# Another order of the same 2043 operations, and another choice of VectorE or GpSimd for them

## The chip, the core and the metric

The kernel runs on one core of a Trainium2 chip. The time is the device time of one execution in microseconds; lower is better. The core has five engines with a queue each: TensorE (PE, with its weight loads shown as PEld), VectorE (DVE), ScalarE (ACT), GpSimd (POOL) and SyncE (SP, which issues the DMAs here). Each runs its own instructions strictly in the order in which the program lists them, and waits on semaphores where it needs another engine's result.

## What is computed

A recurrent attention over 768 tokens (4 batches, 8 heads, head size 40), whose output goes through a soft mixture of 8 experts. All data are float32.

```python
def _attn_ref(r, k, v, w, a, b) -> np.ndarray:
    B, H, S, D = r.shape
    state = np.zeros((B, H, D, D), dtype=np.float32)
    y = np.zeros_like(r)
    for t in range(S):
        ...
        y[:, :, t] = np.einsum('bhd,bhde->bhe', rt, state)
        Sa = np.einsum('bhde,bhe->bhd', state, at)
        state_decay = state * wt[:, :, None, :] - np.einsum('bhd,bhe->bhde', Sa, bt)
        state = state_decay + np.einsum('bhd,bhe->bhde', vt, kt)
    return y.astype(np.float32)

def _moe_ref(x, phi, w1, w2) -> np.ndarray:
    ...
    logits = x @ phi
    d = logits - logits.max(0, keepdims=True)
    d = np.exp(d)
    d /= d.sum(0, keepdims=True) + 1e-09
    slot_input = d.T @ x
    ...
    for e in range(E):
        h = np.maximum(slot_input[e] @ w1[e], 0.0)
        slot_out[e] = h @ w2[e]
    ...
    return (c @ slot_out).astype(np.float32)
```

## The kernel before

The 768 tokens are cut into 12 stages of 64, and every two stages form a pair. Inside a stage the recurrence is turned into matrix products, and only the state goes from stage to stage.

- Preparation of a stage (scan_s, scan_k, scan_c): two scans along the tokens, which VectorE alone can do here, and three 768-wide products of two SBUF operands on either VectorE or GpSimd.
- Grams (lgram, gram, gram_0): TensorE multiplies, VectorE masks the result out of PSUM.
- Solve of a pair (solve_in, solve_step, solve_out): the inverse of triangular 32x32 blocks. VectorE transposes the blocks, ScalarE copies them, and then 30 steps follow, each with a product and a sum over SBUF operands of 30 to 240 elements a partition. Each instruction needs the result of the one before. One buffer (n_a, lt_a) serves all pairs, so a solve starts only after the one before has been transposed out. The first pair is solved in another way (solve_half, VectorE alone); five pairs use solve_step, 300 instructions in all, each on VectorE or GpSimd.
- Chain of a stage (chain_g, chain_u, chain_s): TensorE carries the state on. chain_u of the first stage of a pair needs the solve of that pair (pairs writes it to tbs, of which there is one).
- Output of a stage (y_ut, y_sd, y_p, y_y) and, for each pair, the logits and the running softmax of the experts' slots (slots_a to slots_e); at the end the experts' two products and the output.

The program first records all operations without running them. Then four strings, the result of a search, decide: ORDER gives each recorded operation its place in the program (two digits to base 64 each), and so the order on every engine; PICK gives, for each operation or team of operations that two engines can do, the first or the second of them (VectorE or ScalarE, VectorE or GpSimd); BANK gives each PSUM tile one of eight banks; PACED makes a load wait for another load.

```python
        for os_, c in zip(self.teams(), "".join(PICK)):
            for o in os_:
                o.eng = list(o.alt)[int(c)]
        two = lambda t: [64 * DIGITS.index(t[i]) + DIGITS.index(t[i + 1]) for i in range(0, len(t), 2)]
        rank = two("".join(ORDER))
        self.order = [o for _, o in sorted(zip(rank, self.ops), key=lambda x: x[0])]
```

A step of the solve, as it is recorded:

```python
            nc.both.tensor_tensor(
                tv, n_t[:, 0:i, i:i + 1].broadcast_to([128, i, m]),
                lt[:, i:i + 1, i + 1:].broadcast_to([128, i, m]), ALU.mult)
            nc.both.tensor_tensor(n_t[:, 0:i, i + 1:], n_t[:, 0:i, i + 1:], tv, ALU.add)
```

In the profile every instruction carries the line of emit (L1178), so groups are told apart by engine, operation, tile and shape. A 128x30 to 128x240 TENSOR_TENSOR of wt tiles is a step of a solve; 120x768 is a product of the preparation; 120x780 and 120x781 scans are those of scan_c and scan_s; STREAM_TRANSPOSE is solve_in or solve_out.

Of the kernel before, what the change touches and what calls it, by code (L numbers as in the profile page):

```python
# [124 lines left out]
ORDER = (
    "Cu0203070904100005010F060I0H0G0K0J0E0R0S0A0B0C0V0U0Z0Y0W0X0a0b0h0c0d1d0f0l0e0m0N0L0M0Q1V0O0k0g1a1-1z212O1+2N1j1k"
    "221b1Z0T0i0j0n0o0s0z0u3N1u3K0t0y0p0q0r081P1X1v1q1r0w1f0+0-1l241m1o1t262511122A2C2Z2a2m2b2c2j13140x1i2B2F1g1h0v1c"
    "151628292o2p2n272G1718191A2R0D2T2P2Q0P1n1s2d2e1B1C2x331p2h1D1E1F1G2-1H1I2f2i3D2+3Z1J1K2H2g4S4v1L1M2y1N1O1Q1R2z36"
    "2E2W1S2X2I2l3738393C2J2K2Y3135346T7C5G5v2D2k322w2v4O4Q4M4q3S3o3T3r3A3V4u3B3E5H5u4Y4d5i5tAj631y1Y1e3P3Q3W3X3Y4E3R"
    "2r2L1T2t232U2u3b3p2V4k2q3F3O303j4-3H3L3a4C3U3q3I3J5U3d3e3f3g3c3k4g204h1U4e2M4j1W4i1w6V3h3i3l3m4D4F4I4G4J4H4P3n3s"  # L130
    "4W4b3t3u4f4X4c3v3w3x3y4R4T3z3+4U4n6i3-4041424344454647485N5I5L494A601x6Z6U6a2s565C4K4L3G3M4N4a4l4r4t5l4V4Z6g5O5P"
    "6K5j714m4p4o4w59585B5A575J5k6A4y516O6P6x6w5D5E5M4s4x4z6S7u4B4+50525354555T6G6N5V5W6W6c5y5X5Y6-705Z5a5b5c5R5r5m5q"
    "5n5p5o5d5e696X7B5f5g6m6n6o6p6H6J6q6r6Q6R6s6t6u6v727D7G7H7I686L6Y7f7z6B6E6I78797765675z64615+666b5-2S8B747A6C6D6F"
    "6l6k6j916d88629B9D999G7U7V5K5S5h5x757E7F7N5s5w7M7Q7d9I7L7c5F5Q6M6y6z7R7b7X7Z7a7S7T7i7t767O7g7w737JA0937K7j7y6h6+"
    "7P7h7v8C8R8-6f8H7x8h7e7l9V7+808182837-847m8T9F8F8f7W7Y8S8g8m7k9E8W8i8j8+8d8Y8D856e8789978A8G86APAT9A9+8a8k8l8E95"
    "949890AD92BQBfB1B6BRBS8b8c8e8z8n8p9CAFBcBdBo8V8ZAHA7AAAcAGAd8U8X8oA19JA5ANBp9H9z9w9x9v9yAMALBOBqC1CAA4ACA2AyB0B5"
    "AIAJDoCUCoDqAEAKAW9-A8A9BHBI7n7o7p7q7r7s8I8J8K8LDtDuEb8M8N8O8P8Q8q8r8sAhAxAm96AO8t8u8v8w8x8y9K9LA3A-9M9N9O9P9Q9R"
    "9S9TAXAaAbAYAZAtAv9U9WABA+Be9X9Y9Z9aEhEoEqGY9b9c9d9e9f9g9h9i9j9kB9BA9l9mA6AV9n9o9p9q9r9s9t9uBlBtBuBsBmAwAzB8EREc"
    "IXB-C0BDBEBPIYJHKnNjBMBUBLASARAiAeAqArAfApAQAoCZB3BKBNBYBZAUCcAkCdAnCaAlEOEPBbBnB4BFAsAuBTBVBWBkBrBgB2B7BhAgBGC+"
    "BiBvB+C3BBBCBJCBCHCGCFCECfC-CCCLC2C7BxByBwC9CzEdBjCICJBXBaC4CvDzCDCTCWCVE0CgCmBzC5DgChD4D2CiD1DnD3DxEKF6CyEGEMEZ"  # L140
    "DrDyD+CKCeE9EBECETEVEWCbE5CYCXE6E1E8E3D-FaFRE+FAEAEFEHE7FcE2FdE4FeFYENEQF7FKELEXD0DpCxD5EIESEUFEEyF1GEDsDvFGEkEn"
    "GzFFFHCwDwEDEEEJEgEuGIEfEtEwExF2EvFJFCFDF8GGGPEYElEsFBEiEjFyFzH4GkGlGvH2F3F4F5EaEmEeEpErC6C8CMCNCOCPCQCRCSCjJ0J8"
    "KACkClCnCpCqCrCsCtFnFxFkFjFhD6D7D8D9DADBDCDDEzF0DEDFDGDHDIDJDKDLF9FIFMFPFQFLFODMDNE-FZFNDODPDQDRJQJRJaJcDSDTDUDV"
    "DWDXDYDZDaDbFUFVDcDdFoG8DeDfDhDiDjDkDlDmG9GMGLGVGNFpF+F-K0JgKgMYG6G7G0G1G4KFKmNVONFwFvGHFWFXFbFlFiFuFtFTFSIHIBGi"
    "GmG2G3GCFsIgFgIhFfIFFmG5GZIzJ6GAGBGJGKGTGUGDGSGaGRFqFrGQITIUJOGFGWH7HAGcGfGgGeGsGoGqGpH3GrINItGnGyG-IvG+H5IxIuGt"
    "GuH6GdGjIKGhGxILIsICIGIJGOGwGXGbHaHBIOIPIQISH+HzIVIWKDIMIaH1H9I-J9JDH8IRJBJEJIJ1J7IZIkIDIfIpIiImIIIqIlIjJkJCJbIc"
    "IwJAIrJtIoJmJiJGInH0J5JTJUIdJ3IyJ4I+J2JMJWJZK4KHKRK-IbIeK1JSJzJyJXK8KqKsJKJNJPJJJVLNJdJhK6K7JeKEJfK2K3KzLKLOJwKM"
    "KJKOKIKPKGK9LULcLdMEMHKZKbKeJLJxJ-JYKNHCHDHEHFHGHHHIHJHKHLMQN9MXHMHNHOHPHQHRHSHTLILYJFJvJsHUHVHWHXHYHZHbHcKKKLHd"
    "HeHfHgHhHiHjHkKtKxKvKyL2L7KwHlHmJ+K5KCHnHoHpHqMxNDNNPiHrHsHtHuHvHwHxHyH-I0KWKlI1I2LRLTI3I4I5I6I7I8I9IAL3L4L9L6L5"
    "LJLXLZNYMINbMZK+LPLSLeLfQ2R8SBSCKTKSKQJjJnJrJqJpJlJuJoKBMgLDL0L8LFLGLHMAMTLxM1L-M3KVKdL1LWKULyLzKaLLLMKXKjKrKuLa"  # L150
    "LhLiM0M6M7M9M8M5M4KYKhMBMSKcKpMLMWMJMKMMLbLgMCKfKkMuMyMjMpLBKiKoLQLVOpMNN8NANBMwMvMPNKNPL+MDNONQNTNJNMNRNSNZMlMk"
    "MrMsMnMqMoMmMtO5O9NHNoNWNXNaLAN-O2O1MhMeLCLEMfMdMbMcM2N7NFNfNLNcNUNdMONCNENlNmPTPUPXNGNINnOGNeNiNpNwOFPbNrNtNvNu"
    "NsOKOOPSPZPdNxOPNqOMPjQ0Q1Q3QINkNyOHNgNhOLLjLkLlLmLnLoLpLqLrLsQOQoR3LtLuLvLwMFMGMRMUOWP3O4O8O0MVMaMzM+M-N0N1N2N3"
    "N4N5N6OZOaObOcOIOVOJOTOSOkOUOROdOeOfOgOhOiPkQEQFQrOjOlOmOnOoOrOsOtOuOvOQPEOwOxOyOzO+O-P0P1P2PLPOPPPgQQQJPDPMPNRC"
    "QHRyRlOYPFPIRKSST1TSODOEP9PAP8OBO6P7OCPmPBP4PGPHIEMiROQcQeQYOXP5PKPYPVPWPfOqP6NzO3N+Q6O7OAPcPtPJPQPaPlPyPzPrPqQG"
    "PpPeQyPvP-PwP+Q4PCPoPsQPQRQ7Q8QWQKQVQNQTQLPRQMQUQ5QDQ+Q-R5QlQnQpQAQbQ9QZQCQBQaQXQdRURNR0R1R9QgQhQjQsR4RARHR7RFRG"
    "QkQmPuQSQvR2QxQqQtRdRLRhRgRjRiRfReQiRIRkR6RJQzRERqRmRuS5SFRDRnRoQuQwRBSOSUSLRbRvS8ThSzSWSjRZS9SERsRwRxS7RaRtSwS6"
    "TFSdSJSKSRSTRRRTS2RSRYRQRPS1RXRcS0TcRrS3R+SDRpSQT9TfSMSPTdQfTXTYPnRMSASHSVSYSXPhPxRzTsR-S4SgSeSlSGSISySNSfSZSbSh"
    "SoSsT0SkSnSiSmTZUMRWUZRVTaUNTbUbTeTgTiTkTzSpSrSuSaScT2TjSqSvSxStS+S-T7T3T4T5T6TtTvU3UYT8TDTETGTITJTATBTHTNTCTOTK"
    "TLTPTQTRTTTUTVTlTmTMTrUBUCUFUHUUUVTWU7U6U4U5U8TnTpTqT+T-UKU9UQURTuTyUAUSUDULTwToTxU0U1UEUIUGUJU2UOUXUWUTUPUaVTVU"  # L160
    "VWUfUgUjUkUlUcUdUeUhUiUmUnUoUpVKUqVBUrUvUyUtUxUwUzU-U+ViV0V4V5UuV1V6V8UsV2V3V9VQVSVRVAVGVbVVVYVLVsVoVpV7VCVFVXVt"
    "VuVwVvVIVOVDVEVJVNVHVMVPVcVaVjVdVeVkVlVZVfVgVhVnVmVqVr"
)
# [1278 lines left out]
```

## Time and profile before

| | us |
|---|---|
| median of 3 runs | 405.3 |
| lowest and highest of them | 404.92, 413.21 |
| the profiled execution | 405.49 |
| its span, first to last instruction | 403.7 |

| engine | busy us | share of the span |
|---|---|---|
| TensorE | 337.1 | 84% |
| VectorE | 295.4 | 73% |
| ScalarE | 189.4 | 47% |
| GpSimd | 199.4 | 49% |

The profiled execution's own time is 1.8 us above its span. The mean granted clock of TensorE was 0.916 of its upper level. Busy shares are means over the whole span; what holds the end is read from the chain of waits and from windows of a stretch.

### The profile page before, as it was taken

How to read it: one execution, taken by the hardware profiler on the slowest of the kernel's cores; microseconds unless marked ns; L12 is line 12 of the kernel's file. 1: busy time of each engine (PE TensorE's matmuls, PEld its weight loads, DVE VectorE, ACT ScalarE, POOL GpSimd, SP SyncE). 2: the span in 40 equal slices, each digit the busy share in tenths (PEclk: the TensorE clock that was granted, in tenths of full speed). 3: DMA queues.
4: the chain of work that ended last, by engine and by line, in shares of the span. 5: the costliest groups of instructions: out<-in, count | busy, mean ns of one | idle time of the engine just before them, and what ended most of it. 6: DMA issues, size and time to landing. Idle time of an engine off the chain costs nothing.

```text
span 403.7 us, 18293 instructions
## 1 busy us (share of the span) xinstructions
PE 337.1 (84%) x8097; PEld 295.6 (73%) x8097; DVE 295.4 (73%) x563; ACT 189.4 (47%) x399; POOL 199.4 (49%) x280
## 2 busy tenths in 40 slices
...
GB/s 186 262 233 113 210 3 97 53 188 147 203 54 107 170 92 120 83 64 229 45 62 145 157 182 237 142 157 232 225 169 248 207 203 208 312 296 13 3 175 215
...
## 3 DMA queue, kind: packets, MB, share of 16 engines
...
## 4 chain that ended last, share of the span: by engine, by line
PE 38%; POOL 31%; DVE 13%; issue 8%; DMA 4%; ACT 2%; SPq 0%; DVEq 0%; POOLq 0%; ACTq 0%
PE ps L1178 38%; POOL wt L1178 31%; DVE wt L1178 11%; DMA wt<-in_kb_dram 3%; ACT wt L1178 1%; DMA wt<-in_ww_dram 1%; ACT mem L1178 1%; DVE ps L1178 1%; DVE mem L1178 1%; DVE mid L1178 0%; SPq L1178 0%; DVE slx L1178 0%; DVE old L1178 0%; ACT mid_r L1178 0%; DMA mem<-in_rd_dram 0%
## 5 line engine op out<-in xcount | busy, mean ns | idle before, releaser
L1178 POOL TENSOR_TENSOR wt<-wt 128x234 f32<-128x234 f32 (+14 forms) x237 | 151.4, 639 | 85.9 <-DVE wt L1178 38.0
L1178 PE MATMUL ps<-wt,wt 120*32 120x96 f32 (+9 forms) x3432 | 149.8, 246 | 32.3 <-POOL wt L1178 17.3
L1178 PEld LDWEIGHTS ps<-wt,wt 120*32 120x32 f32 (+7 forms) x3432 | 134.6, 135 | 42.4 <-POOL wt L1178 17.5
L1178 ACT ACTIVATE wt<-ps 32x320 f32<-32x320 f32 (+1 forms) x129 | 55.4, 429 | 30.5 <-PE ps L1178 28.8
L1178 PE MATMUL ps<-cs_t,wt 120*128 120x120 f32 (+4 forms) x448 | 65.3, 284 | 2.5 <-DVE wt L1178 1.7
L1178 DVE TENSOR_TENSOR wt<-ps,cs_t 128x512 f32<-128x512 f32 (+2 forms) x96 | 56.8, 612 | 10.1 <-PE ps L1178 9.6
L1178 ACT COPY wt<-ps 128x320 f32<-128x320 f32 (+2 forms) x81 | 39.5, 507 | 41.4 <-PE ps L1178 38.3
L1178 PEld LDWEIGHTS ps<-cs_t,wt 120*128 120x128 f32 (+4 forms) x448 | 49.5, 148 | 7.2 <-DVE wt L1178 2.4
L1178 DVE TENSOR_TENSOR_SCAN wt<-wt,wt 120x781 f32<-120x781 f32 (+1 forms) x24 | 46.1, 1926 | 2.2 <-DMA wt<-in_ww_dram 1.6
L1178 PE MATMUL ps<-mem 64*64 64x40 f32 (+2 forms) x648 | 41.1, 253 | 5.0 <-DVE wt L1178 4.0
L1178 PE MATMUL ps<-wt,mem 64*64 64x40 f32 (+3 forms) x1072 | 40.1, 254 | 3.6 <-issue 1.7
L1178 PEld LDWEIGHTS ps<-wt,mem 64*64 64x64 f32 (+3 forms) x1072 | 36.6, 135 | 7.5 <-issue 3.3
L1178 DVE TENSOR_TENSOR wt<-wt 128x108 f32<-128x108 f32 (+19 forms) x91 | 34.3, 377 | 10.0 <-POOL wt L1178 7.6
L1178 POOL TENSOR_TENSOR wt<-wt,wt 120x768 f32<-120x768 f32 x17 | 34.4, 2033 | 9.3 <-DMA wt<-in_aa_dram 4.3
L1178 DVE STREAM_TRANSPOSE wt<-wt 128x1024 f32<-128x1024 f32 x12 | 24.8, 2068 | 18.7 <-POOL wt L1178 17.4
L1178 ACT ACTIVATE wt<-wt,bm_t 120x768 f32<-120x768 f32 (+1 forms) x35 | 29.0, 861 | 12.1 <-POOL wt L1178 4.0
L1178 PEld LDWEIGHTS ps<-mem 64*64 64x64 f32 (+2 forms) x648 | 26.8, 141 | 9.7 <-DVE wt L1178 5.0
L1178 PE MATMUL ps<-mem,wt 40*64 40x64 f32 x1536 | 29.0, 228 | 0.3 <-DVE wt L1178 0.2
L1178 PEld LDWEIGHTS ps<-mem,wt 40*64 40x64 f32 x1536 | 26.4, 142 | 2.7 <-issue 1.2
L1178 ACT COPY mem<-ps 120x480 f32<-120x480 f32 (+4 forms) x45 | 18.1, 408 | 20.6 <-PE ps L1178 11.8
L1178 DVE TENSOR_TENSOR wt<-wt,wt 120x768 f32<-120x768 f32 x20 | 23.8, 1198 | 0.2 <-DMA wt<-in_kb_dram 0.2
L1178 DVE TENSOR_TENSOR ps<-ps,wt 120x480 f32<-120x480 f32 (+1 forms) x30 | 17.8, 602 | 6.7 <-PE ps L1178 6.7
...
## 6 DMA issues: line engine op xcount, KB each, us to landing
...
```

The source lines that it names most:

```text
L1178: nc.gpsimd.memset(ysb, 0.0)
```

## The change

The operations are the same, and so is the program that records them. The four strings are others, found by a search in which VectorE and GpSimd exclude each other where both use SBUF operands. Read against the recorded operations, the choice of engines changes as follows:

| operations that can go to two engines | before | after |
|---|---|---|
| solve_step, VectorE / GpSimd | 63 / 237 | 141 / 159 |
| products of scan_k and scan_c, VectorE / GpSimd | 20 / 16 | 16 / 20 |
| small products of scan_s, VectorE / GpSimd | 8 / 3 | 6 / 5 |
| two products ahead of stage 0 and 1, VectorE / GpSimd | 0 / 2 | 2 / 0 |
| copies out of PSUM and the like, VectorE / ScalarE | 75 / 357 | 51 / 381 |

Of the solve's instructions 109 go from GpSimd to VectorE and 31 from VectorE to GpSimd. Within the five solves the engine changes from one instruction to the next 10, 6, 7, 2 and 17 times before, and 24, 18, 23, 17 and 23 times after.

```diff
 ORDER = (
-    "Cu0203070904100005010F060I0H0G0K0J0E0R0S0A0B0C0V0U0Z0Y0W0X0a0b0h0c0d1d0f0l0e0m0N0L0M0Q1V0O0k0g1a1-1z212O1+2N1j1k"
-    "221b1Z0T0i0j0n0o0s0z0u3N1u3K0t0y0p0q0r081P1X1v1q1r0w1f0+0-1l241m1o1t262511122A2C2Z2a2m2b2c2j13140x1i2B2F1g1h0v1c"
...
+    "G7040800060E6a010M0C05020A0703090B0N0K0D0G0R0T0b0l0m0i0e0p0L0Y1I0f0q1i0v0x0y0u0I0F0J0P0H0O100+0t0c0r0k0S0o0j1715"
+    "1o2B0U0V0s0-0z1214181y2e1O2+161C13191B0Z1Y1W1n1w231A1c1E1G2A2H2X1v1z2P2Z1H1J1r1-2K2S2W2l2r2t1M1N1D1f1d1q2V2k1a1t"
...
 )
 PICK = (
-    "1111111011101011111110111110111111111111101110111111111111111011110110000110111100000010111111111111111101110111"
-    "1110100111101111111111011111111111111111111111111101100111011111111111111111111011111100111111110000100000111111"
-    "0001011111111111101111111111111111111111111111101111111011111011010111001111101111111101111110011001110001000100"
-    "0000011111111111111111110111111111111111111111111111101111101101111011110011101111111111111110111111001111111110"
-    "0010111111111111111111111111111011111111111111111111111111101111110111101111100111000111001011001001111111101110"
-    "0010100001001111111111111111111111111001101011111100101110100101110100111100010010101011011111001111101110110011"
-    "0000001110000"
+    "0101110010101101111111011111111111111010111111111111110111111011101111110111110000011110110100000111001111110111"
+    "0100000101011100011110011101111111101111111111111111101111101111111111011011111011111100111111110110101111000000"
+    "1100001110001110001001111111001110110111111110111111111111110111111111111111111111111111111111111011110010010000"
+    "1111001110000100001011000101000101101011111001111111111111111111111111110111111111111111111111111101001111111111"
+    "0101111001001010000000000001100011101111111100011110111000011111111111111111110101101011111111111101111111100000"
+    "1110001000110000010001110110101001111100101011110001110110011110101111111111010101011111010010111011110001100101"
+    "1000001110110"
 )
 BANK = (
-    "0124330665270356725170002715272651376477011662725022576356353677314002527664236431054353014141760614503307542036"
...
+    "0123032642556636667713201556560431036327414106527427466406422205234437637525166377126617752503677012532211450413"
...
 )
 PACED = (
-    "------------------------------------------------------------------1f--------------------------------------------"
-    "0g------0v--0s--0v0i----------------0s----0y130w1B1F1210--1M181Q0+19120z101J0y11141Z1N111P1E1S1G1D1E1a1R1Z1V1Z1f"
...
+    "----------------------------------------------------------------------------------------------------------------"
+    "--------0b----0m--0v0v----0v0z0q--0b0k------0w171E11--140+1I101A1J0i0i1E111J1J1K1P121Z0y1N1E1M1G1F1V1l1L1a1c1b1Z"
...
 )
```

## Rows read from the trace of the kernel before

**Rows 1.** The page's first part: busy time and share of the span by engine.
```profile
PE 337.1 (84%) x8097; PEld 295.6 (73%) x8097; DVE 295.4 (73%) x563; ACT 189.4 (47%) x399; POOL 199.4 (49%) x280
```

**Rows 2.** The page's chain that ended last, share of the span by engine.
```profile
PE 38%; POOL 31%; DVE 13%; issue 8%; DMA 4%; ACT 2%; SPq 0%; DVEq 0%; POOLq 0%; ACTq 0%
```

**Rows 3.** Windows: stretch, length, busy time of PE PEld DVE ACT POOL, PEclk, DMA.
```profile
60.00:99.40 39.40, 36.80 (x1004) 33.39 (x1004) 31.12 (x59) 24.82 (x51) 30.29 (x47) 1.00 0.51 120
99.40:110.70 11.30, 8.75 (x158) 8.12 (x151) 9.12 (x8) 7.67 (x15) 3.27 (x3) 0.70 0.78 190
110.70:152.60 41.90, 39.37 (x1091) 36.76 (x1079) 34.82 (x60) 24.71 (x51) 33.66 (x50) 0.96 0.43 106
152.60:160.00 7.40, 5.92 (x124) 5.07 (x122) 6.88 (x8) 3.96 (x7) 0.00 (x0) 1.00 0.35 105
160.00:202.40 42.40, 37.73 (x950) 34.24 (x946) 32.50 (x63) 25.61 (x55) 34.14 (x49) 1.00 0.40 107
202.40:209.70 7.30, 4.77 (x136) 4.24 (x140) 6.80 (x8) 4.34 (x8) 0.03 (x1) 0.50 0.04 10
209.70:257.80 48.10, 44.88 (x1044) 41.01 (x1038) 34.82 (x65) 25.91 (x56) 38.23 (x57) 0.90 0.69 185
257.80:267.60 9.80, 7.42 (x140) 6.65 (x144) 8.62 (x13) 5.57 (x10) 0.02 (x1) 0.83 0.43 129
267.60:303.10 35.50, 33.77 (x941) 30.17 (x933) 27.01 (x67) 13.96 (x34) 22.72 (x47) 1.00 0.73 200
```

**Rows 4.** Waits of TensorE, 60 to 303 us: total us, times, longest.
```profile
PE ps L1178 <- DVE wt L1178: 12.4, 8, 6.0
...
PE ps L1178 <- POOL wt L1178: 2.5, 1, 2.5
```

**Rows 5.** Timeline, TensorE: the same 32 matmuls of chain_u in two stages.
```profile
158.02 1.13 PE L1178 MATMUL ps<-wt,mem 64*64 64x40 f32 x32
...
209.81 1.89 PE L1178 MATMUL ps<-wt,mem 64*64 64x40 f32 x32
```

**Rows 6.** Chain that ended last, 84 to 93 us: start, length, what.
```profile
86.31 0.58 POOL wt L1178
86.89 0.07 issue
```

**Rows 7.** Timeline, GpSimd and VectorE, 80 to 89 us.
```profile
80.01 0.62 POOL L1178 TENSOR_TENSOR wt<-wt 128x238 f32<-128x238 f32 x1 [0.52 <-DVE wt L1178]
...
86.72 1.81 DVE L1178 TENSOR_TENSOR_SCAN wt<-wt,wt 120x780 f32<-120x780 f32 x1
...
86.96 1.96 POOL L1178 TENSOR_TENSOR wt<-wt 128x210 f32<-128x210 f32 x1
```

**Rows 8.** Groups by form, GpSimd, all of the span: count, busy us, mean ns, idle before.
```profile
L1178 POOL TENSOR_TENSOR wt<-wt 128x238 f32<-128x238 f32 x19 | 19.1, 1004 | 2.4 <-DVE wt L1178 1.0
...
L1178 POOL TENSOR_TENSOR wt<-wt 128x210 f32<-128x210 f32 x16 | 14.5, 904 | 6.3 <-DVE wt L1178 5.3
...
L1178 POOL TENSOR_TENSOR wt<-wt 128x198 f32<-128x198 f32 x14 | 8.0, 571 | 1.1
```

**Rows 9.** Groups by form, VectorE, 60 to 303.1 us.
```profile
L1178 DVE TENSOR_TENSOR wt<-wt,wt 120x768 f32<-120x768 f32 x17 | 18.4, 1090 | 0.2 <-DMA wt<-in_kb_dram 0.2
L1178 DVE STREAM_TRANSPOSE wt<-wt 128x1024 f32<-128x1024 f32 x8 | 16.5, 2067 | 18.6 <-POOL wt L1178 17.4 <-ACT mem L1178 1.2
...
L1178 DVE COPY mem<-ps 120x480 f32<-120x480 f32 x5 | 3.1, 623 | 0.0
...
L1178 DVE TENSOR_TENSOR wt<-wt 128x198 f32<-128x198 f32 x6 | 2.2, 363 | 0.1
```

**Rows 10.** Timeline, the output's DMA issues.
```profile
385.16 14.64 SPq L1178 DMA_DIRECT2D out_dram<-wt  x24
```

**Rows 11.** Waits of VectorE, 60 to 303 us.
```profile
DVE wt L1178 <- POOL wt L1178: 25.3, 14, 6.9
DVE wt L1178 <- PE ps L1178: 10.4, 12, 2.6
```

More of the change, by code (lines that the diff above doesn't have):

```diff
@@ L131 @@
[L131 to L150, printed above, removed]
@@ L161 @@
-    "VWUfUgUjUkUlUcUdUeUhUiUmUnUoUpVKUqVBUrUvUyUtUxUwUzU-U+ViV0V4V5UuV1V6V8UsV2V3V9VQVSVRVAVGVbVVVYVLVsVoVpV7VCVFVXVt"
-    "VuVwVvVIVOVDVEVJVNVHVMVPVcVaVjVdVeVkVlVZVfVgVhVnVmVqVr"
+    "G7040800060E6a010M0C05020A0703090B0N0K0D0G0R0T0b0l0m0i0e0p0L0Y1I0f0q1i0v0x0y0u0I0F0J0P0H0O100+0t0c0r0k0S0o0j1715"
+    "1o2B0U0V0s0-0z1214181y2e1O2+161C13191B0Z1Y1W1n1w231A1c1E1G2A2H2X1v1z2P2Z1H1J1r1-2K2S2W2l2r2t1M1N1D1f1d1q2V2k1a1t"
+    "1P1Q2E2G2b2n2g1F1L1R1T1U1V2L0g2Y0W2M0Q2x32363B1X1b2q3G1K2a1e1g1j1k2w1m1p2u2-3Q4T4q1s1u22314V4Z1x1+2v202124252y34"
@@ new lines @@
+    "1h2h262R292U2c2z3I3K2J2T303A3C3L5e5r4G4N1l3335383D404K3s4-393r2s373J3U3p3H3O3E3S4L4b4D4I2D2d0h1S1Z3N3W3b3Z3Y3c3j"
+    "2j2o0w2m2C2F0X42492O4F2I3d3k3F3M3f3V4f3h3i3a3v3R3e733m3n3o3q3X3P450n472N4J0d4B0a11282i3u3y46483l413w3-3z433t4C4H"
+    "444E4M4P3T4O4a4R4U4W4Y4X4e4d4g3g4x6M4j4l4u585F5J5L5P5T5X5M5G5V5a5d4v2f5K2p545g6j745R6K5A6G3x4Q4h4m4p6V4A4S6S3+4i"
+    "5x6L6i4c4k4t4r5E4+525059565h5y4y556f7I7O63535I5S4o4w5B606F5i5l5o5s5u5z61665q67696D515U5Z6J6O6Z7A6Q6R6U6Y5Y5f5t5p"
+    "5j625v6d6h4n6x6r6k6q6t6v6z715n6576795w5-7C7F7H7L7N7c7X7i7u646B6I787E6E6N6W7R756-4z575W5Q5k4s5N5c272Q5H6l6p6A6u77"
@@ new lines @@
+    "6b7Z7f7D5D6o6g8l9H8X8t7J7M5O5b5C5m707B7P7Y686C7U7a7l8K7T7v5+6H6P6m6c7h7z7p7x7n807s858S6w7W8J8f7K7g7w8B7-82866n6y"
+    "727r8Z7Q7k6s6e7V7t8F7+89B-8A8R8b8V8Y8I8O7o849Q7m8P7e7q8p979U7b8E8m8r8x9K9C8q8G6X6T7j7G8M8D8C7d7S9J878L929R9Y6+9a"
+    "83889j9dALBWBgARAlDDDG8T8j7y819V9e9kAD8h8n8z8a8gAI8k8+ACA5Ac9E9m8u93908d8o8-9xA1AAA3A7ANAJ9i9r959A9S9IB6AMAZA8AF"
+    "AWAs9W9b9o9tA0AUAY989+AG9u9z8H8N8Q8U8W8c8e8i8s8vB9BDEt8w8y9194999B9D9GAeBIB596BK9L9N9P9T9Z9f9h9lAXAn9q9v9y9-A4A9"
+    "AEAKAbAvAiAmAhAgArAOAQAfBVDJATAVAaAd9c9wA2AjAoAxB8BFBLBNBOBRBUBZApAwBbBeAyBEBhBmBoBrBvB+C4C6C8CICJCLCSBGBcBnD+E2"
@@ new lines @@
+    "L1AkB1BMBSBjJ1L0N6Q2BaBkBpAB9s9OAHB39M9F9g9nCABCBfBxBABPBX9XB0B7AqBHBzA6BiBuC9CRCoDIAPAS9pAtBlBsC1C0AuAzCGA+CMCt"
+    "ByCQA-B4B2BBBJCPCZCVCaCXCfChCwD3BTC3CECTBQBdCNCYCbCeClBYBqBwCkCvCUC+C2CmBtDTDuCWCnEcCqD1DEDBD5D8CzCjDcE7CBCOEVF5"
+    "DNDXDbFLFYDdDqDyDjEDDpCrCsCCD0CHCFCpC7CDCcCxC5CdDKDgDmDQFSDtFOCgElCiE8ENFNFRFjFvD2DSCKDYDoE0E4ErD6DVEfDFDOEkEOF0"
+    "GEFFFZELEUDZDkDfEHESEjEAEbEWEeEPEZEgFCFJExF1F9DvEwG6GdD9EJGkGrFVFrFyGcHHE3EnEuDhD-E5EQEXCuCyC-D4D7DADCDHDLDMIXIv"
+    "MGDPDRDUDWDaDlDnDsFQFoF6DiERDwDxDzE1E6EBEEEGFHFnEKEYEdEiEmEpEvEzF2FKFTFAFEFDFIF4F7FBFdFpF8FMFPFUM7MXMbMwFXFbFgFk"
@@ new lines @@
+    "FqFtFwF+G1G5EaEqGBGGGHGaGIGKGPGUGYGbGfGhGiGxGuHQH0FaFiFuJkHKKcMuETFcFlG2GNQ0Q7QAQqGTGFGMECEoDeE-DrF3EMEIEyGpEhE+"
+    "FGGDGSGXEFGWGOG9EsFWE9GgGlHiHtJMJSFfFmG3GAGjGmGqHBFeFhH6H1H8HCHGHaGLGeFxG8GCG-HOH3H4HLHEH5GtGzGVGsHWIVGQG+HRHFGo"
+    "HSHYFsF-GvISIaHbHxHMGJGnHJHpHfHqIcHZHgHhHcHeHlHwHXHdJPH2H9I4I9HrIEILHkIDHnI0I6IlIgIbGZHmG4GRHVHIG0FzHoHjH7I1JZHv"
+    "IAIGHPI8InIZHTIfHDGwHAKRKXJKJrHNHUGyHuIIIPIUKbKtL8LLHzI3KfHsH+IhKiKzIYJJIBIRIOKFKLM1IkIyJ5I+J2IqIsKjLKLeLtM8IoJ-"
+    "IzJEJIJNJaJLMzMqN5N8NAJ6JAJGIeIuJ7KnLCHyH-I2I5I7ICIFIHIKINNjODQ4IQITIWIdIiIrIxJ0JbK1J3J8IwJ4J9JDJHJRJTJVJYJvK9Jh"
@@ new lines @@
+    "JjJnJsJxJ+K0K4JQJpJiJmJeJXJcK5K7IjKlKaKCKIKNKSPZPvPzQgKYKeKkKrKwK-L3L6L7LAJWJyLELJOsPBLNLPLTLVLWLXLdLfLhLqLpLwLr"
+    "K6KWKuOENtOLRwKmKqKUKoL2R2R6R7RyL5K+KvIMIJIpI-ItImJfJCKEJlJdJFJgKKKZKhMoMtJtK3KDKGJOJUKOKVKyLHLjL9JoJwLlLyLbLkJz"
+    "KBKPLuM6M2L-L+M9MRLDLRL4LQLULxLZLcLzMBMDK2KHLGLOLYMKMYLMKdLILnM0M5MEMyMHMUMOMLMTMMMQLiM4LSLgN3NCNJNwO9MeMvM-KJKM"
+    "KQKALFKgKTK8LBNQLmMjMnN9NGNMKxLaO0PVKpKsJqJuLvLsLoMFMAMfOfOpN1NyMaMhMlN4NKNPNVNfOOPWMWMcM3M+MrNSNaONOlPbNYNvN+Nk"
+    "NgNpNqPNPwQ3NmOuN-O4QjQ8QGQIQLNUO3O7NDNdO2MJMNMPMSMVMZMdMgMiMkQRQlQrMmMpMxN0N7NBNFNIOSOhNHNENeNONRNXNbNhNoNsNuNz"
@@ new lines @@
+    "O1O5O8OBOCOFOKOAOUOMOPOTNlOHOGOROWOYOaOeOkQmQoQsQvOmOoOrOwO-P1P6PCPDPGOXPdPIPLPOPTPXPaPePfPgPiPjPpPsQJQDOiOqP0RC"
+    "QMRTShO+PEPYQyRaReTKNWNTN2NcNiNnNNNLNxOZOcOvP7PRJBMIQWQSPrPyO6OIObOjPkPmPtOJOVMsOxMCOQNrNZP3P8OnOyP2PxQBQ5QFQEQT"
+    "Q9PFPnP5PPQCQKQQPAPKPUPhP+P4QbPoQUQdQhQYQeOdQZQcPcPqQxR0R8Q+RBRJOzP9PJOtPQPHPMP-Q1PlRIQpQuRLQiR4PSQVQXRSRUQ6QOQn"
+    "QfQwQHQaRARERGQNQzR3RiRvRtRxRqS2RpQtR1R5RMRbRZRfRVRQRlRmRzRcR+S6RHRORhSDSRSnRsS1SESISiSPSqQkSFSGRWRYS3S4RnRuSTR-"
+    "T9SrS8SAScSeRDRgRPRFRNRjRrRoRkSZSYSWS5SBSCSOQ-RRTDTZSJSLSaQPSXSbOgPuS7SMSNSUSSR9SdSmUdS9SKSQSfSwSkStT5RXSsSVSjSl"
```

33 lines of the change are left out of this document (12 added, 21 removed).

## The prediction

> **What bounds the kernel now.** I read five views, from the coarse to the fine. The first part of the page [rows 1] has TensorE busy for 84% of the span and no other engine over 73%, so TensorE is the first suspect; but its busy time of 337.1 us is 67 us short of the span, and the question is who makes it idle. The chain of waits [rows 2] gives TensorE only 38%; GpSimd has 31% and VectorE 13%. A step of that chain on GpSimd means that the end of the program hangs on work that GpSimd can't do earlier. That work is the solve (solve_step): 30 steps of two instructions, each needing the one before, once per pair of stages, five times with an engine to choose (300 instructions).
>
> The windows cut at the first and last instruction of each solve [rows 3] show where it sits: five stretches of 39.4, 41.9, 42.4, 48.1 and 35.5 us, 207.3 in all, and 35.8 us of transposes, copies and preparation between them. From 60.0 to 303.1 us one solve follows another without a break. In the same 243.1 us TensorE is busy 219.4 us (the nine rows summed) and VectorE 191.7 us, 79%. TensorE's waits in that stretch [rows 4] are 12.4 us for VectorE's wt tiles, 6.0 at once, and 2.5 for GpSimd's. The 6.0 us fall at the end of the third solve, where VectorE's transpose can't start until GpSimd's last step. So the solve is the pace-maker by a small margin over TensorE, not by a large one.
>
> There is a second cost of the same stalls. The granted clock [rows 3] falls to 0.70 after the first solve, to 0.50 after the third, 0.90 in the stretch behind it and 0.83 after the fourth; a mean of 0.70 is a share of 0.6 of the time at the lower of the two levels (1.2 instead of 2.4 GHz), and the same reading of the other rows gives 6.8 + 3.4 + 7.3 + 9.6 + 3.3 = 30 us at 1.2 GHz, each time behind a stop of TensorE. What that costs is in two rows of the same 32 matmuls of chain_u: 1.13 us at the upper level, 1.89 at the lower [rows 5]. Some 5 of the 30 us are idle anyway; the other 25 do work of 25 x 1.13 / 1.89 = 15 us, so the low clock costs about 10.
>
> **Why the solve is slow.** In the chain of waits the step at 86.31 takes GpSimd 0.58 us [rows 6]; the next one, of the same 128x210, begins at 86.96 and takes 1.96 [rows 7]. Under the long one lies a scan on VectorE (two SBUF inputs) from 86.72 to 88.53; GpSimd's instruction, begun 0.24 us after it, ends 0.39 after its end. A form of 128x238 with nothing of that kind beside it takes 0.62 [rows 7]. So the two exclude each other for a whole instruction when both read SBUF. The groups by form [rows 8] carry the sum: with 0.6 us for a free one, the means of 1004 and 904 ns over 19 and 16 instructions are 7.7 + 4.9 = 12.6 us of standing still; the other long forms (220 to 240, and 168) bring the same reading to about 30 us. Without them the five solves would need some 177 us, not 207.
>
> **The change part by part.** Read digit by digit against the recorded operations, the new PICK moves 109 solve instructions from GpSimd to VectorE and 31 back: GpSimd 237 to 159, VectorE 63 to 141. 65 of the net 78 are of the six forms of 210 to 240 elements. A form that both engines run undisturbed gives the price: 128x198 is 571 ns on GpSimd and 363 on VectorE [rows 8, 9], 0.21 less. 65 x 0.21 + 13 x 0.16 (the smaller forms save less, an estimate from the same two rows scaled by size) = 16 us off the five solves. Against it stands a change of engine inside a solve: 42 now, 105 then. A step on the same engine follows after 0.07 us [rows 6]; a hop leaves about 0.07 more where VectorE is free, so 63 x 0.07 = 4 us. Net 12.
>
> The blocked 30 us. The new order can't abolish exclusion: the scans (1.8 us each, two a stage) and the 768-wide products of eight stages must still run during these 243 us, and the new ORDER lists about 29 us of such work between the first and last steps of the five solves (the scan's 1.8 and the products' 0.95 us counted up). Such work adds to the chain on whichever engine it is, but each instruction once, and a step that would have stood still on GpSimd can run at VectorE's price behind it. Bounds: nothing saved (0), all saved (30). I take half, 15, because the scans need a place and the stretches between the solves are not empty either: in the first of them GpSimd is busy for 3.3 of 11.3 us and VectorE for 9.1 [rows 3]. So the solves would go from 207 to some 180 us.
>
> That much can't come out at the end, because TensorE takes over. Its floor in the middle stretch is 219.4 less the 10 of the clock, and the waits that solves cause are 12.4 + 2.5 = 14.9; so at most 25 us are to be had, which is 380.5 against the profiled 405.5.
>
> What VectorE loses: 78 x 0.38 = 30 us more solve work (0.36 at 198 elements, a little more above), less the 768-wide products that go to GpSimd in this stretch, a net six (1.09 us each in the mean [rows 9], of which I take 0.95 as undisturbed), less a net dozen of evacuations moved to ScalarE (0.62 us for the 120x480 copy [rows 9]), 7 us: 191.7 + 30 - 6 - 7 = 209, or 201 without the blocking that VectorE itself suffers now. In a stretch of 230 us that is 87 to 91%, against 79. ScalarE takes those copies free, being at 47% [rows 1], and so far the cover of the evacuations is that VectorE had 50 us spare. With 25 spare some of them come late, and TensorE, which issues in order, waits for its PSUM bank. I therefore count two thirds of the waits (10 of 14.9) as gone, and of the clock's 10 a third (3), since a few stops are enough to drop it again: 13 us.
>
> The remaining parts I cost at nothing, within bounds. BANK, the TensorE order and the pace of the loads change everywhere, but the cumulative TensorE work ahead of each chain_u differs by 11 us at most, both ways, and the number of instructions on TensorE is the same. In the prologue GpSimd gives two 768-wide products to VectorE and two more loads go ahead of the first a tile: -2 to +3 us, an estimate from one such product saved (1.7 against 0.95) and one load displaced. At the end SyncE's 24 output issues take 14.64 us [rows 10], so the end hangs on when the first starts; it now wants four matmuls and copies instead of two, while the last stack is out of the way: -1 to +1.
>
> Sum against the profiled execution: 405.5 - 13 = 392.5. The median of the runs shown is 405.3, 0.2 lower, so I say 392.
>
> **Rivals.** First, *time about as now, 398 to 407*: VectorE takes the place of GpSimd as the engine behind which the chain queues. For it: 105 hops, and a step that arrives at VectorE must let the instruction in service finish (a mask of 0.68 us, a scan of 1.8). With 52 entries and 0.3 us each that is 16 us, which eats what the shorter steps gave; the blocked time saved then ends in about 400. Against it: VectorE's list for each solve is no longer than the solve itself. The page Perfetto Trace Analysis of the Trainium skill, section Optimizing Scalar/DVE Operations, speaks for this case: work moved between these two engines might not help, as they share a read port. By that rule a moved step saves nothing and the sum would be near 403; the pair of rows for 128x198 speaks against it, since the same step holds the port 0.21 us less on VectorE.
>
> Second, *slower, about 413*: VectorE stands still in front of a solve step while evacuations queue behind it. It is in order, so on each entry into VectorE it waits for GpSimd's last step (0.25 to 0.62 us). Now it waits 25.3 us for GpSimd in 14 places [rows 11], 17.4 of them ahead of transposes [rows 9], where nothing is lost by it; and some 20 us for TensorE (10.4 in the largest row). Its 205 us of work plus 20 leave 18 of the 243. 52 entries reach that at 0.35 us each; from there every further tenth costs 5 us, and at 0.5 us, a whole middling step, the stretch is 8 us longer than now: 405.5 + 8 = 413.
>
> Third, *380 to 385*: TensorE is never let down and the clock stays at 2.4 GHz.
>
> **How the numbers follow.** The forecast case, 386 to 397, gets 0.55; about as now 0.25; slower 0.12; the floor 0.08. A 2% bound (397 to 413 counts as the same; less can hardly be told from no change with this spread of runs) gives faster 0.63, same 0.25, slower 0.12. The range of 383 to 408 leaves out the slower case and half of the floor case, 0.16.
>
> **What would show it.** Right: solve stretches of 33 to 39 us, means of the 210 to 240 forms on GpSimd near 0.65 us, VectorE at 85% or more from 60 us on, and GpSimd's share of the chain of waits under 20% with TensorE's over 50%; no clock row at 0.5 between 100 and 300 us. Wrong: long forms on GpSimd still near 0.9 us (exclusion not avoided), or TensorE's waits for VectorE over 15 us with VectorE waiting for GpSimd in many short pieces (the second rival).

## The result and the profile after

The changed kernel takes 388.35 us in the median of 4 runs (385.29 to 394.12), beside 406.43 (404.92 to 413.21) of the kernel before on the same chip; the ratio is 0.954, 95% interval 0.945 to 0.963. It is faster, and some 4 us more so than the forecast of 392. Some executions of one kernel are slower at a lower granted clock: the ratios and their intervals leave these out, and where the profiled execution of an experiment below is one of them (x5, x2, x3, e3), its rows serve for the mechanism and not for a few us.

The profiled execution took 388.45 us with a span of 386.1, against 405.49 and 403.7. First the page's busy times, which answer to [rows 1]:

```profile
PE 331.3 (86%) x8097; PEld 286.7 (74%) x8097; DVE 289.2 (75%) x613; ACT 199.6 (52%) x423; POOL 138.8 (36%) x206
```

TensorE runs the same 8097 matmuls in 5.8 us less, and its share of the span grows. GpSimd loses 60 us. VectorE has 50 instructions more and yet 6 us less busy time over the span: short steps came, longer copies and products left, and less of it stands still. In the middle stretch, shown below, it has 6.9 us more to do.

The windows, cut at the first and last instruction of each of the five solves as in [rows 3]: stretch, length, busy time of PE PEld DVE ACT POOL, PEclk, DMA.

```profile
0.00:59.10 59.10, 35.83 (x1014) 32.23 (x1014) 48.41 (x78) 24.95 (x44) 22.85 (x20) 0.83 0.71 185
59.10:95.60 36.50, 34.73 (x923) 31.47 (x924) 32.41 (x71) 22.94 (x49) 21.01 (x34) 1.00 0.56 123
95.60:106.50 10.90, 10.15 (x312) 9.11 (x306) 10.29 (x13) 9.11 (x18) 5.67 (x3) 1.00 0.50 130
106.50:143.90 37.40, 36.73 (x930) 32.63 (x927) 34.14 (x72) 24.38 (x53) 24.47 (x37) 1.00 0.47 112
143.90:152.70 8.80, 8.54 (x242) 7.66 (x242) 8.29 (x9) 6.47 (x13) 3.38 (x2) 1.00 0.64 173
152.70:188.40 35.70, 34.62 (x890) 31.69 (x888) 32.02 (x74) 25.04 (x51) 18.02 (x33) 1.00 0.55 136
188.40:202.50 14.10, 13.51 (x378) 12.24 (x378) 13.90 (x13) 10.95 (x26) 6.88 (x6) 1.00 0.64 157
202.50:242.70 40.20, 36.56 (x924) 33.30 (x923) 32.30 (x73) 21.06 (x44) 17.76 (x34) 0.96 0.63 160
242.70:250.80 8.10, 7.62 (x220) 6.33 (x217) 7.25 (x10) 6.80 (x13) 0.04 (x1) 1.00 0.77 240
250.80:285.00 34.20, 32.36 (x794) 28.22 (x796) 27.99 (x74) 14.90 (x35) 15.33 (x34) 1.00 0.79 209
285.00:386.20 101.20, 80.62 (x1507) 61.83 (x1507) 42.22 (x138) 32.99 (x81) 3.40 (x6) 0.85 0.60 177
```

The five solve stretches are 36.5, 37.4, 35.7, 40.2 and 34.2 us, 184.0 in all, where they were 207.3. The middle of the kernel, all nine rows of it, shrinks from 243.1 to 225.9 us, and that 17.2 is the whole gain (17.6 in the span): the part before the first solve is 0.9 shorter, the part behind the last 0.5 longer. One row per kernel for the whole middle stretch splits the 17.2, of before:

```profile
60.00:303.10 243.10, 219.41 (x5532) 199.63 (x5529) 191.68 (x346) 136.55 (x286) 162.36 (x251) 0.94 0.54 140
```

and of after:

```profile
59.10:285.00 225.90, 214.83 (x5578) 192.66 (x5580) 198.59 (x399) 141.64 (x298) 112.57 (x180) 0.99 0.60 151
```

TensorE's idle time there (length less busy) goes from 23.7 to 11.1 us, 12.6 less, and its busy time falls by 4.6 at a clock of 0.99 instead of 0.94, although 46 more matmuls fall into the stretch. TensorE's waits in this stretch, total, times and longest, which answer to [rows 4]:

```profile
PE ps L1174 <- issue: 4.5, 6, 2.2
PE ps L1174 <- ACT wt L1174: 2.7, 8, 0.5
...
PE ps L1174 <- POOL wt L1174: 0.6, 1, 0.6
PE ps L1174 <- DVE wt L1174: 0.6, 1, 0.6
```

The 14.9 us behind VectorE's and GpSimd's tiles have become 1.2. In the page's chain of waits GpSimd no longer appears:

```profile
PE 33%; ACT 3%; issue 2%; DVE 1%; DMA 1%; DVEq 0%; SPq 0%; ACTq 0%
```

Before it held 31% [rows 2]. The shares add up to 40% because this chain was followed back only as far as 213 us, so it says nothing of the first three solves; of what it covers, TensorE has four fifths.

### The profile page after: what moved, and what is told of

Read it like the earlier page. It is cut to its first block, busy times and chain, and to the rows that moved or that the text cites. A ratio compares the mean times of both kernels' runs of the same rounds, so it can differ in the third digit from the quotient of the medians.

```text
span 386.1 us, 18326 instructions
## 1 busy us (share of the span) xinstructions
PE 331.3 (86%) x8097; PEld 286.7 (74%) x8097; DVE 289.2 (75%) x613; ACT 199.6 (52%) x423; POOL 138.8 (36%) x206
## 5 line engine op out<-in xcount | busy, mean ns | idle before, releaser
L1174 PE MATMUL ps<-wt,wt 96*32 96x40 f32 (+8 forms) x3432 | 143.4, 240 | 24.1 <-ACT wt L1174 16.8
L1174 PEld LDWEIGHTS ps<-wt,wt 120*32 120x32 f32 (+6 forms) x3432 | 128.1, 130 | 33.4 <-issue 25.0
L1174 POOL TENSOR_TENSOR wt<-wt 128x84 f32<-128x84 f32 (+14 forms) x159 | 92.0, 579 | 102.4 <-DVE wt L1174 78.7
L1174 PE MATMUL ps<-cs_t,wt 120*128 120x120 f32 (+4 forms) x448 | 62.3, 273 | 2.9 <-DVE wt L1174 0.7
L1174 DVE TENSOR_TENSOR wt<-wt 128x240 f32<-128x240 f32 (+17 forms) x169 | 56.6, 335 | 9.8 <-POOL wt L1174 5.2
L1174 ACT COPY wt<-ps 128x320 f32<-128x320 f32 (+2 forms) x86 | 41.5, 508 | 43.3 <-PE ps L1174 42.0
L1174 PEld LDWEIGHTS ps<-cs_t,wt 120*128 120x128 f32 (+4 forms) x448 | 46.1, 140 | 9.4 <-ACT wt L1174 2.3
L1174 DVE TENSOR_TENSOR_SCAN wt<-wt,wt 120x781 f32<-120x781 f32 (+1 forms) x24 | 43.1, 1798 | 2.2 <-DMA wt<-in_ww_dram 1.9
L1174 ACT COPY mem<-ps 120x480 f32<-120x480 f32 (+4 forms) x56 | 23.1, 427 | 23.9 <-PE ps L1174 21.7
L1174 ACT ACTIVATE mem<-wt,cs_t 128x512 f32<-128x512 f32 x21 | 14.3, 716 | 11.1 <-DVE wt L1174 10.9
```

Source lines behind the costliest of these rows:

```text
L1174: nc.vector.memset(inj_f, 0.0)
```

## The experiments

All times are medians; each ratio is to runs of the kernel before on the same chip, with its 95% interval. The changed kernel itself stands at 0.954 (0.945 to 0.963). Where the text counts single steps of the solve, they were matched to the trace in program order.

### Does the solve pace the kernel, before and after?

**Shorter steps, before and after** (x5 and x6). One edit in both kernels:

```diff
-            m = 31 - i
+            m = (34 - i) // 4
...
-                lt[:, i:i + 1, i + 1:].broadcast_to([128, i, m]), ALU.mult)
-            nc.both.tensor_tensor(n_t[:, 0:i, i + 1:], n_t[:, 0:i, i + 1:], tv, ALU.add)
+                lt[:, i:i + 1, i + 1:i + 1 + m].broadcast_to([128, i, m]), ALU.mult)
+            nc.both.tensor_tensor(n_t[:, 0:i, i + 1:i + 1 + m], n_t[:, 0:i, i + 1:i + 1 + m], tv, ALU.add)
```

> The kernel before, in which each step of the solve multiplies and adds only the first quarter of its columns (values not computed; the steps, their engines and their order stay). Theory A, the solve paces TensorE: with steps of 8 to 60 elements, some 0.25 us shorter each, the middle stretch ends where TensorE allows, and the time falls to 382 to 391. Theory B, it is the order on TensorE, its banks and loads that held the kernel before: the solves get shorter, but the time stays at 399 to 406.

> The changed kernel with the same quarter steps. Theory A, the change has taken the solve out of the way and TensorE paces (11 us of gaps left in the middle stretch): 381 to 388, at most 7 us less. Rival C, the solve still paces after the change, only faster: 365 to 380, as each of 300 steps loses some 0.15 to 0.25 us.

Before with short steps: 383.27 us (379.38 to 389.36), ratio 0.928 (0.919 to 0.937). After with short steps: 392.66 us (389.35 to 393.82), ratio 0.957 (0.950 to 0.964), which is the changed kernel's own 0.954 within the intervals; the time lies some 5 us above the range that I had given. The same medicine is worth 7% in one kernel and nothing in the other. The middle stretch of before with short steps is 15.7 us shorter than in [rows 3], and its idle time on TensorE falls to 10.2:

```profile
58.70:286.10 227.40, 217.20 (x5545) 198.60 (x5542) 179.30 (x346) 136.30 (x286) 109.08 (x251) 0.94 0.58 150
```

The same row of after with short steps shows no such thing, although GpSimd works 37.6 us less and VectorE 20 us less than in after:

```profile
58.90:289.40 230.50, 219.85 (x5578) 197.68 (x5579) 178.45 (x398) 141.62 (x298) 75.01 (x180) 0.96 0.58 148
```

Where did nearly 60 us of shorter work go? Its solves still take 180.2 us, and the trace shows it in one place. GpSimd's queue in the timeline of after with short steps (start, length, what, in brackets the wait before it):

```profile
114.38 0.57 POOL L1174 TENSOR_TENSOR wt<-wt 128x28 f32<-128x28 f32 x2 [0.39 <-DVE wt L1174]
120.16 0.27 POOL L1174 TENSOR_TENSOR wt<-wt 128x42 f32<-128x42 f32 x1 [5.22 <-DVE wt L1174]
```

and VectorE's in the same 6 us:

```profile
115.75 0.55 DVE L1174 TENSOR_TENSOR wt<-ps,cs_t 96x384 f32<-96x384 f32 x1 [1.45 <-PE ps L1174]
116.22 1.77 DVE L1174 TENSOR_TENSOR_SCAN wt<-wt,wt 120x781 f32<-120x781 f32 x1
119.08 0.67 DVE L1174 TENSOR_TENSOR ps<-ps,wt 120x480 f32<-120x480 f32 x1 [1.09 <-PE ps L1174]
119.66 0.43 DVE L1174 TENSOR_TENSOR wt<-wt 128x35 f32<-128x35 f32 x2
```

GpSimd ends its step at 114.95. The next two steps are VectorE's, but in its queue a mask, a scan and an operation on PSUM stand ahead of them, and the first and the last of the three wait for TensorE (1.45 and 1.09 us). They begin at 119.66, 4.71 later. Part of that is VectorE's own work, so one place doesn't settle who sets the pace; the sums do. VectorE's waits for TensorE in the middle stretch add up to 16.2 us in after and to 37.6 here, so the 20 us of work that VectorE lost became waiting for TensorE. The largest of these rows:

```profile
DVE wt L1174 <- PE ps L1174: 20.0, 22, 3.1
```

And the page's chain of after with short steps, which here covers nearly the whole span, has no GpSimd in it:

```profile
PE 74%; ACT 8%; DVE 7%; issue 4%; DMA 2%; DVEq 0%; SPq 0%; ACTq 0%
```

So in the changed kernel the solve goes at the pace of TensorE. Over all changes from GpSimd to VectorE such gaps add up to 17.5 us in after and to 70.1 with short steps: what the steps save, the gaps take up. The mechanism of theory A holds on both sides.

**Scans that don't exclude GpSimd, before and after** (x1 and x2). The same edit in both, for stages 4 to 11 counted from 0, which is from the fifth stage on:

```diff
-            nc.vector.tensor_tensor_scan(
...
+            if st > 3:
+                nc.vector.transpose(s_t[0:96, 0:768], w_t[0:96, 0:768])
+            else:
+                nc.vector.tensor_tensor_scan(
...
-            nc.vector.tensor_tensor_scan(ct, ct, inj_f, 0.0, ALU.mult, ALU.add)
+            if st > 3:
+                nc.vector.transpose(ct[0:96, 0:768], ct[0:96, 0:768])
+            else:
+                nc.vector.tensor_tensor_scan(ct, ct, inj_f, 0.0, ALU.mult, ALU.add)
```

> The kernel before, in which the two scans of each stage from the fifth on are replaced by a transpose of 96x768 in the same place (about as long, one SBUF input instead of two), so the values of these stages are not computed. Theory A (a VectorE instruction with two SBUF inputs holds up GpSimd for its whole length, one with a single input does not): the long forms on GpSimd fall from 0.9 to 1.0 us to 0.65 to 0.75, the solves from 207 to 183 to 190 us, the time to 390 to 396. Rival (GpSimd's long instructions have another cause, as the length of VectorE's work or the queue): means stay near 0.9 and the time within 402 to 407, less at most the 3 us by which the transposes are shorter.

> The changed kernel with the scans of all stages from the fourth on replaced by a 96x768 transpose in place, which does not hold GpSimd up (values not computed). Theory A: the 18.6 us of steps that still stand still on GpSimd lie mostly beside a busy TensorE, so 382 to 388. Rival C, the solve still paces: 370 to 380.

Before without these scans: 391.4 us (386.28 to 399.64), ratio 0.955 (0.945 to 0.965), as much as the whole change. Its solves sum to 190.2 us, 16.9 less than before, and the time that solve steps stand still on GpSimd (each step over the shortest of its form, where over 0.15) falls from 31.5 to 14.4 us. The groups by form of GpSimd in the first four solves show where:

```profile
L1184 POOL TENSOR_TENSOR wt<-wt 128x238 f32<-128x238 f32 x15 | 13.6, 907 | 2.1 <-DVE wt L1184 1.0
...
L1184 POOL TENSOR_TENSOR wt<-wt 128x210 f32<-128x210 f32 x14 | 8.8, 628 | 6.2 <-DVE wt L1184 5.3
```

The form of 210, 949 ns in the mean of the same four solves before (904 over all five, [rows 8]), is down to 628; that of 238 falls from 1102 to 907 only, for it still meets the 768-wide products, and so does that of 228, which got longer (716 to 850). Of the 32 steps of GpSimd that are blocked before, 13 have a scan of VectorE beside them and 17 a 768-wide product; of the 17 that are blocked here, 16 have a product beside them and none a transpose. One reservation: the transpose takes 0.96 us where the scan took 1.8, so VectorE is relieved by some 13 us as well; but it was not the engine that ended the solves, and the solves' 16.9 us agree with the 17.1 that no longer stand still.

After without these scans: 389.68 us (383.87 to 391.08), ratio 0.944 (0.932 to 0.956). The expectation gave 382 to 388, somewhat less than was measured; against the changed kernel's 0.954 the intervals overlap, so there is a gain of at most some per cent and none that can be told from nothing, and rival C's 370 to 380 is excluded. Its middle row:

```profile
61.40:289.90 228.50, 219.59 (x5601) 197.85 (x5602) 186.11 (x397) 141.91 (x298) 98.60 (x180) 0.96 0.58 150
```

8.9 us of idle TensorE remain. The steps now stand still for some 5.5 us on GpSimd instead of 18.8, but the gaps at changes from GpSimd to VectorE go from 17.5 to 35.1 us and the five solves sum to 186.3 us, no less than in after (183.5). So what still stands still on GpSimd in after stands in time that the solve has to spare.

### Which part of the change carries it?

**The solve's engines and the order apart** (e1, e2, e4). The first is the changed kernel, in which the solve steps take the engine that they had before:

```diff
-        for os_, c in zip(self.teams(), "".join(PICK)):
+        for os_, c, c2 in zip(self.teams(), "".join(PICK), "".join(OTHER)):
+            c = c2 if os_[0].who.startswith("solve_step") else c
```

with OTHER the PICK of the kernel before. The second is the same edit in the kernel before, with OTHER the PICK after. The third is the changed kernel's ORDER, BANK and PACED with the whole PICK of the kernel before.

> The changed kernel, with the engine of each solve_step instruction as before (237 on GpSimd, 63 on VectorE) and all else as changed. Theory A (the gain is the solve: cheaper steps and fewer of them standing still): the steps alone cost 17 us more over the five solves and more of them meet VectorE's scans; the solves go from 184 to 205 us or more, the time to 398 to 406. Theory B (the gain is the new order of TensorE, banks and loads, and the solve had room): 386 to 391, solves longer but TensorE not waiting.

> The kernel before, with the changed engines of the solve_step instructions (159 on GpSimd, 141 on VectorE) and the order, the other engines, banks and loads as before. Theory A: the cheaper steps are there, but the order of VectorE's queue was not made for them, so some stand behind other work: solves of 195 to 205 us, 397 to 404. If the choice of engines alone is the gain: 389 to 394. Theory B: 403 to 408, no gain without the new order.

> The changed kernel's order, banks and load pace with the whole choice of engines of the kernel before. Theory A, order and engines work only together: 405 to 430, no better than before. Theory B, order, banks and loads alone carry the gain: 386 to 395.

They took 416.97 us (414.18 to 419.65; ratio 1.027, 1.017 to 1.036), 482.67 us (482.21 to 484.08; 1.189, 1.181 to 1.197) and 426.16 us (421.97 to 429.82; 1.037, 1.028 to 1.046). Neither part gives anything alone, and each alone costs; the whole new choice of engines in the old order was not run, for e2 moves the solve's steps only. I had expected the first at 398 to 406 and was 11 us short; for the second I had expected a gain, and it lost 77 us. The theory that order, banks and loads carry the gain falls with e4.

In e1 the solves take 206.5 us, as before, and the stretch is longer than before:

```profile
60.30:315.80 255.50, 233.57 (x5600) 208.75 (x5602) 170.62 (x320) 141.82 (x298) 157.37 (x258) 0.91 0.53 136
```

Against the row of after, 5600 matmuls instead of 5578, TensorE idles 10.9 us more (21.9 to 11.1), but its busy time grows by 18.7, at a clock of 0.91 instead of 0.99. The stops themselves are the smaller part of the loss.

In e2 the solves get shorter (197.3 us in all, two of them 31.4 and 28.4), and the stretch from the first to the last grows by 73 us. VectorE's waits from 61 to 378 us, and TensorE's:

```profile
DVE wt L1188 <- POOL wt L1188: 68.7, 46, 5.2
```

```profile
PE ps L1188 <- DVE wt L1188: 34.4, 5, 18.3
PE ps L1188 <- issue: 24.1, 7, 21.3
```

VectorE's queue, in the old order, reaches its new steps long before GpSimd has done the ones ahead of them, and stands still 46 times, 1.5 us each; behind it wait the masks and copies that TensorE needs, 18.3 us at once. In after VectorE waits for GpSimd for only 5.6 us, in 11 places; of the 25.3 us before [rows 11], 17.4 stood ahead of transposes [rows 9]:

```profile
DVE wt L1174 <- PE ps L1174: 8.4, 11, 1.6
DVE wt L1174 <- POOL wt L1174: 5.6, 11, 1.0
```

**The other engines** (e3, and its two halves e6 and e7): the same edit in the changed kernel, for every operation that is not a solve_step; for the products of scan_s, scan_k and scan_c alone (with them goes one copy in scan_c); and for the rest, which is the other copies and the two products ahead of stage 0 and 1.

> The changed kernel, with the engines of all operations other than solve_step as before (copies between VectorE and ScalarE, products of the preparation between VectorE and GpSimd). Theory A: VectorE gets back some 17 us of work in the middle stretch, where it is busy for nine tenths, and evacuations come later: 389 to 395. If these copies are covered: 387 to 390. Theory B has nothing on it.

> The changed kernel with the engines of the kernel before for the preparation's products alone (scan_s, scan_k, scan_c). Theory A, the 768-wide products on the wrong one of the two engines stand in the solve's way: 394 to 405, they carry most of the loss seen when all other engines were set back. Rival, the copies carry it: 386 to 392 here.

> The changed kernel with the engines of the kernel before for the copies out of PSUM and the like alone (VectorE or ScalarE; 24 more on VectorE, some 12 us of work at 0.3 to 0.7 each). Theory A: VectorE has about 15 us to spare in the middle stretch, so 388 to 394. Rival, copies on VectorE at the wrong place hold TensorE's banks: 396 to 408.

e3 took 406.84 us (399.38 to 411.31), for which no ratio can be given, against 405.61 of the kernel before on the same chip. It missed both expectations. e6 took 390.78 us (387.18 to 393.03), ratio 0.969 (0.951 to 0.987): the rival's range, and hardly apart from the changed kernel. e7 took 403.6 us (395.79 to 406.26), ratio 0.991 (0.978 to 1.004): the rival's range again. So it is the choice for the copies that matters (93 of them change their engine in e7, in the changed kernel a net 23 to ScalarE), together with the two products, which no run parts from them; and here I was wrong twice. The middle row of e7:

```profile
64.00:298.20 234.20, 219.51 (x5691) 197.17 (x5689) 204.69 (x412) 135.60 (x283) 111.20 (x180) 0.98 0.57 146
```

VectorE has only 6.1 us more to do in it than after (204.7 of 234.2 us), still 13% spare, and yet the stretch is 8.3 us longer. 4.7 of that is TensorE's own work, as 113 more matmuls fall into the stretch, and 3.6 its idle time; its waits for VectorE's tiles go from 0.6 us to

```profile
PE ps L1184 <- DVE wt L1184: 4.3, 7, 0.9
```

The stretch also starts 4.9 us later; whether that is the two products' part stays open. So VectorE's spare time can't be counted as cover: 13% of it left, and TensorE waits for its tiles in more places.

**All steps on one engine** (x4 and x3): the changed kernel with `c = "0"` (VectorE) or `c = "1"` (GpSimd) for every solve_step.

> The changed kernel with all 300 solve steps on VectorE: no change of engine and no step of GpSimd's left to block. Theory A, VectorE becomes the bound: 159 steps of about 0.3 us more make 199 + 48 = 247 us of work in a stretch of 226, so 408 to 425. Rival C, changes of engine and blocked steps were what still held the kernel: 375 to 386.

> The changed kernel with all 300 solve steps on GpSimd: VectorE loses some 50 us of work. Theory A, the solve paces again, as each of 141 steps gets 0.2 us longer and GpSimd's steps stand still beside more of VectorE's work (30 us or more): solves of 42 to 48 us and 405 to 425. Rival, VectorE's load is what holds the kernel after: 380 to 390.

All on VectorE: 413.66 us (411.77 to 422.09), ratio 1.030 (1.017 to 1.044). All on GpSimd: 413.45 us (406.51 to 414.75), again without a ratio. The middle rows, VectorE's first:

```profile
60.60:311.40 250.80, 227.36 (x5632) 200.74 (x5632) 239.67 (x556) 141.54 (x297) 21.95 (x21) 0.97 0.53 136
```

```profile
60.80:313.30 252.50, 231.92 (x5616) 208.99 (x5618) 157.82 (x258) 141.84 (x298) 190.37 (x321) 0.91 0.53 135
```

With all on VectorE there are no changes of engine and no step that another engine blocks, and VectorE is busy for 239.7 of 250.8 us; TensorE waits for its tiles 21 times:

```profile
PE ps L1175 <- DVE wt L1175: 14.1, 21, 1.8
```

With all on GpSimd VectorE has 95 us to spare, and the solve paces again; the page's chain gives GpSimd the largest share:

```profile
POOL 38%; PE 36%; issue 8%; DVE 8%; ACT 6%; DMA 2%; SPq 0%; DVEq 0%; ACTq 0%; POOLq 0%
```

There the solves sum to 197.8 us (34.9 to 42.2, less than the 42 to 48 each that I had expected) and the transposes and waits between them to 54.7; the steps stand still for some 21 us, not 30 or more. In the order that was made for the new division, both ends of the choice cost 6 to 8% against the changed kernel (413.45 / 408.69 and 1.030, over 0.954); the division 141 to 159 lies between a VectorE that is full and a GpSimd that is slow.

## Why the prediction was right

**The bound.** The solve by a small margin over TensorE: shown. Quarter steps took 7% off the kernel before and nothing off the changed one.

**Exclusion.** That a scan and a GpSimd step exclude each other, and that it costs the solves about 30 us, of which half can be saved: the steps stood still for 31.5 us on GpSimd and 3.9 on VectorE before, 18.8 and 0 after, so 16.6 less where I took 15. Half was a choice between none and all, so that it came this close is luck. With the scans replaced by an instruction that doesn't exclude, 17 us of standing still went, and 17 of the solves. But I had expected all forms of 210 to 240 elements near 0.65 us on GpSimd, and that was wrong for four of the six; the prediction itself had named means near 0.9 as a sign of being wrong. GpSimd's groups by form in after, of which three stand here, and a form that is not blocked:

```profile
L1174 POOL TENSOR_TENSOR wt<-wt 128x220 f32<-128x220 f32 x11 | 13.1, 1191 | 11.3 <-DVE wt L1174 11.0
...
L1174 POOL TENSOR_TENSOR wt<-wt 128x198 f32<-128x198 f32 x13 | 7.4, 566 | 10.2 <-DVE wt L1174 9.6
...
L1174 POOL TENSOR_TENSOR wt<-wt 128x210 f32<-128x210 f32 x9 | 6.8, 753 | 4.4 <-DVE wt L1174 3.9
...
L1174 POOL TENSOR_TENSOR wt<-wt 128x238 f32<-128x238 f32 x6 | 5.2, 863 | 8.9 <-DVE wt L1174 8.8
```

The new sequence doesn't avoid exclusion; it has fewer blocked steps (14 instead of 32; e1, the old engines in the new order, has 14 as well), at places where x2 shows them to cost nothing that can be measured.

**The steps.** 0.21 us saved per long step: after has 566 ns on GpSimd for 128x198 and 360 on VectorE:

```profile
L1174 DVE TENSOR_TENSOR wt<-wt 128x198 f32<-128x198 f32 x7 | 2.5, 360 | 0.2
```

The busy time of the 300 steps falls from 177.0 to 141.9 us; less the 16.6 of standing still that is 18.5, for the 16 that I had worked out. The Trainium skill's page Perfetto Trace Analysis, section Optimizing Scalar/DVE Operations, says that moving work between these two engines might not help, as they share a read port. For these steps the trace shows the other case: each takes 0.21 us less on VectorE. In x4, where all of them were moved, the time got longer, but there VectorE was full. The 403 that the prediction put beside that rule doesn't follow from its other terms: without the 16 us the solves would still lose 11 of 27, and in proportion the time would be about 400.

**The changes of engine.** This is the term that I mis-sized: 4 us counted, 11.5 measured. The gaps at such places go from 10.2 us in 42 to 22.8 in 105, 12.6 more, and those between steps on one engine fall by 1.1. A change into VectorE doesn't cost a fixed 0.07: half of the 53 take 0.03 us, and 15 that are over 0.3 us make up 15.5 of the 17.5 us; they cost what stands in VectorE's queue. It did no harm, as x6 shows: those gaps are slack once TensorE sets the pace. In all the solves lost 23.6 us, not 27: 183.5 measured from the first step's start to the last one's end, where I had said some 180.

**What TensorE gives back.** I allowed 25 us at most and counted 13: 10 of its waits and 3 of the clock. It was 12.6 of idle time and 4.6 of busy time, both terms a little too small; that is why the result is 388 and not 392. That the clock's term came out near is partly luck. With one row at 0.96 and all others in the middle at 1.00, the few stops that I thought would drop the clock again did not come: read as in the prediction, the middle's time at 1.2 GHz falls from 30 to 3 us, and not by a third. At the price of [rows 5] that is worth some 10 us (an estimate), not 3; of this only 4.6 show in the stretch, at least in part because 46 more matmuls fall into it.

**VectorE's load.** Worked out as 201 to 209 us and 87 to 91%; measured 198.6, 88%. That it leaves time for the evacuations was right in the sum, but the reason was wrong: I had counted the copies given to ScalarE as so much less work for VectorE, and e7, which sets them back (with the two products) and loses most of the gain, shows that more hangs on them than that sum.

**The rivals.** About as now, through waits in VectorE's queue: those waits are there, 17.5 us of them, and hidden. Slower, through a VectorE that stands still in front of the solve: not in this order (5.6 us), but exactly so in the old one (68.7 us, e2). The floor of 380 to 385: not reached by the changed kernel, nor by x2 or x6, whose TensorE still idles 9 to 11 us; the kernel before with short steps comes to 383. Why the old TensorE order is the better one by 2 to 3% when the solve is light (x5 against x6, on one chip) stays open.

**The ends.** The prologue (-0.9, within -2 to +3) and the tail (+0.5, within -1 to +1) were as bounded. For the tail, two things that I had not counted cancel. The part behind the last solve, before:

```profile
303.10:403.80 100.70, 81.73 (x1648) 63.79 (x1646) 50.28 (x144) 30.37 (x76) 3.41 (x6) 0.92 0.62 187
```

After, 141 fewer matmuls fall into it, but its clock is 0.85 instead of 0.92, which by the same reading is 14 us more at 1.2 GHz. So half of the low clock that left the middle came back here.
